# Grouping small tiled matmuls: state reads of two or three batches at once, and W1 pieces as one stream across batches, three at a time in the second group

## The chip, the cores and the metric

The kernel runs on one core of one Trainium2 chip. The metric is device time in microseconds (us) of that core, as a median of several executions. "Span" is the length of the one execution that the profiler recorded; it is a little shorter than the timed runs. In the profiles PE is TensorE, PEld its weight loads, DVE VectorE, ACT ScalarE and POOL GpSimd. A bank is one of the PSUM buffers into which TensorE writes; an eviction is another engine's copy out of it, after which the bank is free again.

## The reference, cut to what matters

```python
# x: (B=8, H=8, S=512, D=64), state: (8, 8, Ns=32, 64), w_in: (512, 2048), w_out: (2048, 512)
a     = softmax(x @ state^T / 8)            # per batch and head, 512 x 32
xread = a @ state                           # 512 x 64
a2    = softmax(state @ x^T / 8)            # 32 x 512
sread = a2 @ x                              # 32 x 64: the "state read"
y     = concat([xread, sread], axis=2)      # (8, 8, 544, 64), heads then joined to 512 columns
h     = y @ w_in                            # 4352 x 2048
out   = (h * sigmoid(h)) @ w_out            # 4352 x 512
```

For the rows of `xread`, the kernel never forms `xread`. It forms `W1 = state @ w_in` for each batch (256 x 2048, once the heads are stacked) and then `h = a @ W1`. Making W1 is one small job per batch, and the state read is another. Both use small pieces of the TensorE array. The state reads are kept until the end, where one last block of 256 rows goes through `w_in` and `w_out`.

## The kernel before

The parts that the change and the argument touch (cuts marked):

```python
    psO = ... tile_pool(name="psO", bufs=1, PSUM)     # o0, o1
    psH = ... tile_pool(name="psH", bufs=2, PSUM)     # h1, twice
    psA = ... tile_pool(name="psA", bufs=1, PSUM)     # a0..a3, given out in turn by bank()

    def sread(bs):                    # state read: 32 matmuls of 65 columns for each batch
        ps = psH.tile([128, 512], FP32, tag="h1", name="ps_sr")
        for i, b in enumerate(bs):
            xm_ps[b] = ps[:, ds(132 * i, 132)]
            for hg in range(2):
                for c in range(4):
                    for s in range(4):
                        # ... cut
                        nc.tensor.matmul(
                            xm_ps[b][ds(32 * s, 32), ds(66 * hg + odd, 65)],
                            exp_nat[b, hg][:, c, s, :],
                            x_rows[b % NX][:, ds(at, 65)],
                            start=(c == 0), stop=(c == 3),
                            tile_position=(0, 32 * s), skip_group_check=True)

    def sread_out(b):                 # its eviction: 4 reciprocals and a product on DVE
        # ... cut

    def w1_mms(b, cols, new=bank):    # one piece is 512 columns of W1: 8 matmuls into 2 banks
        # ... cut
        for f, n in cols:
            for hg in range(2):
                pss[f, hg] = new([128, 512], FP32, "ps_w1")
            for s in range(4):
                for hg in range(2):
                    h = HEAD_OF_SLOT[hg][s]
                    r = 64 * (h % 2)
                    nc.tensor.matmul(
                        pss[f, hg][ds(32 * s, 32), 0:n],
                        stT[ds(r, 64), b, h // 2, s % 2, :],
                        w_in_sb[ds(r, 64), h // 2, ds(f, n)],
                        start=True, stop=True,
                        tile_position=(r, 32 * s), skip_group_check=True)
        return pss

    for b in range(1, B):
        n = b + 1
        m = n + 1
        # ... cut
        for tt in range(4):           # 4 blocks of 128 rows
            for ft in range(NFT):     # 16 steps of G2: o += g @ w_out, a full-size matmul
                at = (tt, ft)
                # ... cut: the h matmuls (G1), loads, casts, transposes
                if n < B and at == (1, 6 if b == 1 else 4):     # the first group
                    if m < B:
                        scores_t(m)
                    pss = w1_mms(n, [(0, 512), (512, 512)])
                    sread((0, 1, 2) if b == 1 else (n,))
                    if m < B:
                        exps_t(m)
                        nc.scalar.activation(warm[:], busy[:, 0:1], func=SILU, bias=0.0)
                    w1_out(n, [(0, 512)], both, pss)
                    for i in (0, 1, 2) if b == 1 else (n,):
                        sread_out(i)
                    w1_out(n, [(512, 512)], both, pss)
                # ... cut
                if n < B:
                    if at == (2, 8):                            # the second group
                        w1_chunks(n, (2, 3), both)
                # ... cut
                G2(b, tt, ft)
```

So each of batches 1 to 6 interrupts the full-size matmuls twice. The first group is eight transposed score matmuls (64 x 32 pieces of the array), two W1 pieces (64 x 32 as well) and a state read (128 x 32 pieces). Batch 1 reads three batches at once, and batch 6 has no scores. The second group is two W1 pieces.

The softmax here doesn't subtract the row's maximum and nothing guards it: scores larger than these inputs give would overflow.

## Time and profile before

| | before |
|---|---|
| time, median of 3 runs | 214.66 us (214.51 to 214.76) |
| span of the profile | 212.8 us |
| PE busy | 97% |
| ACT, DVE busy | 66%, 36% |

From the profile's page of the kernel before, part 1 (busy us, share of the span, instructions) and part 4 (the chain of work that ended last, by engine and then by line):

```profile
PE 206.4 (97%) x1575; PEld 96.6 (45%) x1575; DVE 77.0 (36%) x171; ACT 139.4 (66%) x244; POOL 39.9 (19%) x62
...
PE 90%; DVE 4%; DMA 2%; ACT 2%; issue 0%; SPq 0%
```

The chain is TensorE almost throughout. Whatever shortens the stream of TensorE shortens the kernel, and a lighter DVE or ACT alone does not.

The next lines are from the timeline of PE in the kernel before. The columns are start, length, engine, line, operation, output and inputs, array pieces used, shape, and count of the merged run. The first block holds both groups of batch 2 with the full-size matmuls around them; after it come only the marks at which the groups of the next batches begin.

```profile
70.75 2.32 PE L559 MATMUL o<-w_out_sb,g 128*128 128x512 bf16 x10
73.00 0.41 PE L330 MATMUL ps_scT<-xT,stT 64*32 64x512 bf16 x8
73.23 0.62 PE L464 MATMUL ps_w<-w_in_sb,stT 64*32 64x512 bf16 x16
73.77 0.43 PE L416 MATMUL ps_sr<-x_rows,e 128*32 128x65 bf16 x32
74.14 4.49 PE L559 MATMUL o<-w_out_sb,g 128*128 128x512 bf16 x20
78.56 0.62 PE L464 MATMUL ps_w<-w_in_sb,stT 64*32 64x512 bf16 x16
79.11 2.12 PE L559 MATMUL o<-w_out_sb,g 128*128 128x512 bf16 x9
...
95.62 0.41 PE L330 MATMUL ps_scT<-xT,stT 64*32 64x512 bf16 x8
...
118.24 0.41 PE L330 MATMUL ps_scT<-xT,stT 64*32 64x512 bf16 x8
...
140.86 0.41 PE L330 MATMUL ps_scT<-xT,stT 64*32 64x512 bf16 x8
```

Read starts, not lengths. Matmuls are pipelined, so the length of a run includes the last one's latency and overlaps what follows: a single full-size matmul is recorded with 0.38 us, though the next starts 0.216 us after it. Full-size matmuls start 0.216 us apart. The ten that begin at 70.75 would be followed by another at 70.75 + 10 x 0.216 = 72.91. Instead the scores start at 73.00 and the next full-size matmul at 74.14, so the first group takes 1.23 us out of the stream. The twenty from 74.14 end their turn at 78.46, W1 starts at 78.56 and full-size matmuls are back at 79.11, so the second group takes 0.65 us. Two W1 pieces need only 2 x 0.216 = 0.43 us of array time, as the eight matmuls of a piece run side by side (the eight scores, of the same shape, take 73.00 to 73.23).

A second place matters, batch 1, where three batches are read together and the second group waits. From the timelines of PE and then of DVE in the kernel before:

```profile
46.13 0.59 PE L518 MATMUL h<-aT,W 128*128 128x512 bf16 x2
46.56 0.63 PE L304 MATMUL ps_sc<-stT,xT 128*128 128x64 bf16 x16
47.03 2.32 PE L559 MATMUL o<-w_out_sb,g 128*128 128x512 bf16 x10
...
50.15 0.96 PE L416 MATMUL ps_sr<-x_rows,exp_nat 128*32 128x65 bf16 x96
51.04 4.06 PE L559 MATMUL o<-w_out_sb,g 128*128 128x512 bf16 x18
55.03 0.41 PE L464 MATMUL ps_w<-w_in_sb,stT 64*32 64x512 bf16 x8
56.11 0.41 PE L464 MATMUL ps_w<-w_in_sb,stT 64*32 64x512 bf16 x8 [0.68 <-DVE W L158]
```

```profile
51.97 0.68 DVE L158 CAST W<-ps_w 128x512 bf16<-128x512 f32 x1
52.57 0.69 DVE L432 RECIPROCAL rc<-ps_sr 32x2 f32<-32x2 f32 x4
...
55.17 0.29 DVE L433 TENSOR_TENSOR xm<-ps_sr,rc 128x128 bf16<-128x128 f32 x1
55.38 0.68 DVE L158 CAST W<-ps_w 128x512 bf16<-128x512 f32 x1
```

Three reads together took 50.15 to 51.04 = 0.89 us, a single one 73.77 to 74.14 = 0.37 us. So a batch costs 0.26 us and the read as such 0.11 us. The bracket on the last PE line says that PE sat idle for 0.68 us until a DVE eviction freed a bank. Measured by starts, 55.03 + 0.216 = 55.25 was the due time and 56.11 the real one: 0.86 us lost. Small matmuls that use the *whole* array (scores of batch 2, 128 x 64) start exactly where the next full-size one was due (46.13 + 2 x 0.216 = 46.56). There is no gap ahead of them.

### The profile page before, as it was taken

How to read it: one execution, taken by the hardware profiler on the slowest of the kernel's cores; microseconds unless marked ns; L12 is line 12 of the kernel's file. 1: busy time of each engine (PE TensorE's matmuls, PEld its weight loads, DVE VectorE, ACT ScalarE, POOL GpSimd, SP SyncE). 2: the span in 40 equal slices, each digit the busy share in tenths (PEclk: the TensorE clock that was granted, in tenths of full speed). 3: DMA queues.
4: the chain of work that ended last, by engine and by line, in shares of the span. 5: the costliest groups of instructions: out<-in, count | busy, mean ns of one | idle time of the engine just before them, and what ended most of it. 6: DMA issues, size and time to landing. Idle time of an engine off the chain costs nothing.

```text
span 212.8 us, 3896 instructions
## 1 busy us (share of the span) xinstructions
PE 206.4 (97%) x1575; PEld 96.6 (45%) x1575; DVE 77.0 (36%) x171; ACT 139.4 (66%) x244; POOL 39.9 (19%) x62
## 2 busy tenths in 40 slices
PE   7899999999899999999999999999999999999993
PEld 2443354445344434444444444443444444466653
DVE  3851268738921255115610661045212406100011
ACT  3865677899377876697669955995776366644410
POOL 8682116405120402021200301000200000000000
PEclk9999999999999999999999999999999999999999
DMA  5999999993469358454756573115311111011112
GB/s 189 195 207 204 286 261 350 286 284 108 85 157 270 125 114 163 124 158 108 194 79 219 79 180 99 49 52 105 99 49 46 62 49 54 0 49 49 52 49 99
DMA packets 42930, 28.66 MB, mean 135 GB/s; under 512 B 28064, under 2 KB 37792, under 8 KB 42912
## 3 DMA queue, kind: packets, MB, share of 16 engines
q1 hardware_dynamic: 36720, 20.65, 36.8%
q0 software_dynamic: 5904, 7.64, 17.3%
q8 instruction: 12, 0.20, 0.4%
q10 hardware_dynamic: 288, 0.13, 0.2%
q14 instruction: 6, 0.05, 0.1%
HBM read 17.43 MB, written 8.91 MB: 124 GB/s over the span
## 4 chain that ended last, share of the span: by engine, by line
PE 90%; DVE 4%; DMA 2%; ACT 2%; issue 0%; SPq 0%
PE o L559 48%; PE h L518 26%; PE ps_w L464 4%; PE h L539 3%; PE o_a L559 3%; DMA x_f<-in_x_dram 2%; PE o_part L581 2%; DVE W L158 1%; PE ps_sr L416 1%; DVE rc L432 1%; PE ps_scT L330 1%; PE ps_busy L164 1%; ACT L318 1%; DVE rs L377 1%; ACT exp_nat L318 1%; PE ps_at L396 0%
## 5 line engine op out<-in xcount | busy, mean ns | idle before, releaser
L559 PE MATMUL o<-w_out_sb,g 128*128 128x512 bf16 x496 | 132.2, 379 | 0.0
L550 ACT ACTIVATE g<-h 128x512 bf16<-128x512 f32 (+1 forms) x143 | 81.3, 573 | 35.3 <-PE h L518 21.2
L559 PEld LDWEIGHTS <-g 128*128 128x128 bf16 x528 | 50.0, 98 | 57.9 <-issue 3.2
L518 PE MATMUL h<-aT,W 128*128 128x512 bf16 x254 | 74.7, 379 | 0.1
L158 DVE COPY o_sb<-o 128x512 f32<-128x512 f32 x15 | 10.4, 691 | 89.5 <-PE o L559 80.9
L518 PEld LDWEIGHTS <-W 128*128 128x128 bf16 x254 | 24.5, 98 | 30.6 <-issue 1.2
L158 DVE CAST W<-ps_w 128x512 bf16<-128x512 f32 (+2 forms) x36 | 22.7, 658 | 26.3 <-PE ps_w L464 26.3
L156 ACT ACTIVATE W<-ps_w 128x512 bf16<-128x512 f32 (+1 forms) x32 | 16.6, 561 | 12.6 <-PE ps_w L464 12.6
L158 POOL CAST x_nat<-x_f 128x512 bf16<-128x512 f32 x24 | 14.5, 646 | 33.6 <-issue 21.7
L156 ACT ACTIVATE o_sb<-o 128x512 f32<-128x512 f32 x16 | 9.5, 596 | 13.2 <-PE o L559 10.0
L360 POOL TENSOR_TENSOR an<-e,rcn 128x512 bf16<-128x512 bf16 x5 | 7.6, 1517 | 50.0 <-DVE rcn L358 50.0
L464 PE MATMUL ps_w<-w_in_sb,stT 64*32 64x512 bf16 (+2 forms) x264 | 10.8, 375 | 0.7 <-DVE W L158 0.7
L559 PE MATMUL o_a<-w_out_sb,g 128*128 128x512 bf16 x32 | 10.0, 379 | 0.0
L539 PE MATMUL h<-xmT,w_in_sb 128*128 128x256 bf16 x64 | 9.6, 273 | 0.0
L539 PEld LDWEIGHTS <-w_in_sb 128*128 128x128 bf16 x64 | 6.3, 98 | 3.9
L164 PE MATMUL ps_busy<-busy 128*128 128x512 bf16 x16 | 5.9, 487 | 1.2 <-DVE warm L171 1.2
L344 ACT ACTIVATE eT<-ps_scT 128x512 bf16<-128x512 f32 x10 | 5.4, 594 | 1.6 <-PE ps_scT L330 1.6
L769 ACT ACT_TABLE_LOAD x5 | 6.4, 1283 | 0.1
L464 PEld LDWEIGHTS <-stT 64*32 64x32 bf16 x264 | 3.1, 89 | 7.0 <-issue 5.1
L380 POOL TENSOR_TENSOR an<-exp_nat,rc 128x512 bf16<-128x512 bf16 x3 | 3.1, 1047 | 15.7 <-ACT eT L344 9.9
L357 DVE TENSOR_REDUCE rs<-e 128x32 f32<-128x1024 bf16 x5 | 6.0, 1207 | 0.0
L432 DVE RECIPROCAL rc<-ps_sr 32x2 f32<-32x2 f32 x32 | 5.2, 164 | 0.3
(76 smaller groups left out, 103.7 us busy)
## 6 DMA issues: line engine op xcount, KB each, us to landing
out_dram<-o_sb SPq DMA_DIRECT2D x33, 256.0 KB, 2.5
x_f<-in_x_dram SPq DMA_DIRECT2D x4, 1024.0 KB, 6.0
x_f<-in_x_dram POOLq DMA_DIRECT2D x2, 1024.0 KB, 11.7
w_in_sb<-in_moe_w_in_dram POOLq DMA_DIRECT2D x3, 512.0 KB, 9.9
x_f<-in_x_dram SPq DMA_DIRECT2D x2, 512.0 KB, 4.8
w_out_sb<-in_moe_w_out_dram POOLq DMA_DIRECT2D x4, 256.0 KB, 11.8
w_out_sb<-in_moe_w_out_dram POOLq DMA_DIRECT2D x2, 512.0 KB, 11.9
x_f<-in_x_dram POOLq DMA_DIRECT2D x2, 512.0 KB, 14.6
```

Source lines behind the costliest of these rows:

```text
L156: nc.scalar.activation(dst, src, func=COPY, bias=0.0)
L158: eng.tensor_copy(dst, src)
L164: nc.tensor.matmul(ps[:], busy[:, 0:128], busy[:], start=True, stop=True, skip_group_check=True)
L357: nc.vector.tensor_reduce(rs[:], e2[b][:], axis=AX, op=ADD)
L360: eng.tensor_tensor(a[:, hg], e2[b][:, hg], rc[:, hg].to_broadcast([128, 4, 4, NS]), op=MULT)
L432: nc.vector.reciprocal(rc[q, :], src)
L464: nc.tensor.matmul(pss[f, hg][ds(32 * s, 32), 0:n], stT[ds(r, 64), b, h // 2, s % 2, :], w_in_sb[ds(r, 64), h // 2, ds(f, n)], start=True, ...
L518: nc.tensor.matmul(h_ps[k][:], W1[b][:, hg, ds(128 * ft, 128)], aT[b][:, hg, :, :], start=(hg == 0), stop=(hg == 1), skip_group_check=True,)
L539: nc.tensor.matmul(ps[:, 0:256], w_in_sb[:, kt, ds(128 * ft, 128)], xmT[:, :, kt].rearrange("p t n b -> p t (n b)"), start=(kt == 0), stop ...
L550: nc.scalar.activation(g[:, 0:n], ps[:, 0:n], func=SILU, bias=0.0)
L559: nc.tensor.matmul(outs[tt][:], gt[b * NFT + ft][:, ds(128 * tt, 128)], w_out_sb[:, ft, :], start=(ft == 0), stop=(ft == NFT - 1), skip_gr ...
L769: nc.scalar.activation(warm[:], busy[:, 0:1], func=SILU, bias=0.0)
```

## The change

The intent is to interrupt the full-size stream less often for the same small work. The 24 W1 pieces of batches 2 to 7 are made as one queue, two in every first group and three in a second group, so that only four batches need a second group. The third piece takes the two `h1` banks. The state reads of batches 3 to 7 are done as 3, 4, 5 in batch 4 and 6, 7 in batch 6. One more `e2` buffer keeps the exponentials until then.

```diff
+SREAD_AT = {1: (0, 1, 2), 4: (3, 4, 5), 6: (6, 7)}
 ... cut
-    e2pool = ctx.enter_context(tc.tile_pool(name="e2pool", bufs=3))
+    e2pool = ctx.enter_context(tc.tile_pool(name="e2pool", bufs=4))
 ... cut
+    pieces = [(i, [(512 * c, 512)]) for i in range(2, B) for c in range(4)]
+
+    def w1_next(k, new=bank):
+        done = []
+        for _ in range(k):
+            i, cols = pieces.pop(0)
+            done.append((i, cols, both, w1_mms(i, cols, new)))
+        return done
 ... cut
-                    pss = w1_mms(n, [(0, 512), (512, 512)])
-                    sread((0, 1, 2) if b == 1 else (n,))
+                    pss = w1_next(2)
+                    srs = SREAD_AT.get(b, ())
+                    if srs:
+                        sread(srs)
 ... cut
-                    w1_out(n, [(0, 512)], both, pss)
-                    for i in (0, 1, 2) if b == 1 else (n,):
+                    w1_out(*pss[0])
+                    for i in srs:
                         sread_out(i)
-                    w1_out(n, [(512, 512)], both, pss)
+                    w1_out(*pss[1])
 ... cut
-                    if at == (2, 8):
-                        w1_chunks(n, (2, 3), both)
+                    if at == (2, 8) and b in (1, 2, 4, 5):
+                        pss = w1_next(2) + w1_next(1, new_h)
+                        for i in (2, 0, 1):
+                            w1_out(*pss[i])
```

## The prediction

> **What bounds the kernel.** TensorE. The page gives PE 97% of the 212.8 us span, and the chain that ended last is 90% PE. In the timeline of PE, batches 1 to 6 repeat every 22.6 us (the eight score matmuls start at 73.00, 95.62, 118.24, 140.86). Full-size matmuls start 0.216 us apart, so the 96 of a batch (32 for h, 64 for o) take 20.74 us. The other 1.89 us are two interruptions by tiled matmuls. ACT (66%) and DVE (36%) have slack, and the granted clock is full, so only PE's own stream is worth counting.
>
> **Prices, from the timeline of PE in batch 2.** Group one: the next full matmul was due at 72.91; scores start 73.00, W1 73.23, state read 73.77, full matmuls again at 74.14: 1.23 us. Group two: due 78.46, W1 starts 78.56, full again 79.11: 0.65 us for two W1 pieces. A piece is eight matmuls of 512 columns that run side by side, so 0.216 us. That leaves, as estimates from these numbers, 0.10 us to enter a group and 0.11 us to leave it, about 0.21 us per group. A state read of one batch is 0.37 us; in batch 1 three batches read together take 0.89 us (50.15 to 51.04), so 0.26 us per batch and 0.11 us once per read, for the change of tile shape. The Trainium skill, "TensorEngine Tiling (Array Packing)", section Key Properties, says that changing the tiling mode drains TensorE; these gaps agree with it.
>
> **What the change does.** No matmul is added or removed: still 24 W1 pieces in batches 1 to 6 and eight state reads.
> - Group two goes from six times two pieces to four times three (batches 1, 2, 4, 5). Batches 3 and 6 lose it: -2 x 0.65 = -1.31 us. Four groups gain a piece: +4 x 0.216 = +0.86 us. Net -0.44 us.
> - The reads of batches 2, 3 and 5 go (-3 x 0.37 = -1.11 us); batch 4 reads three and batch 6 two (+3 x 0.26 = +0.78 us). Net -0.33 us.
> - Sum -0.77 us, all on PE and so all on the chain.
>
> **What could collide.** Three read evictions on DVE in batch 4 take about 2.8 us (0.94 each) and hold back the second W1 eviction. Estimated from batch 5's times it ends about 4.8 us after the group begins; group two begins 5.56 us after, so nothing waits. In batch 1 it does wait (W1 at 55.03, second half at 56.11 behind a DVE eviction, about 0.86 us lost); neither the order nor the banks there change, so I expect that loss to stay. The third piece uses the two h banks, evicted first, before h wants them about 2 us later. The fourth e2 buffer lets batch 6's exponentials be written while batches 3 to 5 wait; no new wait.
>
> **Prediction.** 213.9 us, range 213.4 to 214.5 (about -0.36%). Faster by over 2%: 0.5%; within 2%: 99%; slower by over 2%: 0.5%.
>
> **What would show it.** Batch 3's period about 0.37+0.65 = 1.0 us shorter (21.6 us); batch 6 about 0.4 shorter; batches 2 and 5 0.15 shorter; batch 4 longer by 0.52+0.22 = 0.74; batch 1 longer by 0.22. Read of three in batch 4 takes 0.89 us. Third piece 0.216 us. Batch 1's wait for DVE stays near 0.7 to 0.9 us.
>
> **What would make it wrong.** A W1 stall in batch 4 like batch 1's (+0.3 to 0.9 us, the gain gone); the third piece in the h banks waiting for the read's eviction, or h waiting for the piece's; or the batch 1 stall vanishing (0.8 us more gain). If the drain depends on what is in flight, each of five saved switches may be worth 0 to 0.2 us rather than 0.11 to 0.21.

## The result and the profile after

| | before | after |
|---|---|---|
| median | 214.58 us (the 3 runs above and one more) | 213.89 us (4 runs, 213.73 to 214.01) |
| ratio, 95% interval | | 0.9967 (0.9949 to 0.9984) |
| span of the profile | 212.8 us | 212.0 us |

The change is within 2%, but the interval lies wholly below 1.

From the profile's page of the kernel after, parts 1 and 4:

```profile
PE 206.1 (97%) x1575; PEld 96.9 (46%) x1575; DVE 77.3 (36%) x171; ACT 139.2 (66%) x244; POOL 39.5 (19%) x62
...
PE 92%; DVE 4%; ACT 1%; issue 0%
```

PE has 1575 matmuls in both kernels, and its busy share is unchanged, though 0.8 us of span are gone. The saving was made of gaps that the busy figure hardly shows. In the matmul records of the two traces, the array's shape changes 30 times in the six batches before and 23 times after.

From the timeline of PE in the kernel after, batch 2, then the first group of batch 3, then both groups of batch 4:

```profile
70.93 2.32 PE L560 MATMUL o<-w_out_sb,g 128*128 128x512 bf16 x10
73.18 0.41 PE L331 MATMUL ps_scT<-xT,stT 64*32 64x512 bf16 x8
73.41 0.61 PE L465 MATMUL ps_w<-w_in_sb,stT 64*32 64x512 bf16 x16
73.96 4.49 PE L560 MATMUL o<-w_out_sb,g 128*128 128x512 bf16 x20
78.38 0.84 PE L465 MATMUL ps_w<-w_in_sb,stT 64*32 64x512 bf16 x24
79.15 2.12 PE L560 MATMUL o<-w_out_sb,g 128*128 128x512 bf16 x9
...
95.66 0.41 PE L331 MATMUL ps_scT<-xT,stT 64*32 64x512 bf16 x8
95.88 0.61 PE L465 MATMUL ps_w<-w_in_sb,stT 64*32 64x512 bf16 x16
96.43 6.43 PE L560 MATMUL o<-w_out_sb,g 128*128 128x512 bf16 x29
...
117.25 0.41 PE L331 MATMUL ps_scT<-xT,stT 64*32 64x512 bf16 x8
...
118.03 0.96 PE L417 MATMUL ps_sr<-x_rows,e 128*32 128x65 bf16 x96
118.92 4.49 PE L560 MATMUL o<-w_out_sb,g 128*128 128x512 bf16 x20
123.34 0.84 PE L465 MATMUL ps_w<-w_in_sb,stT 64*32 64x512 bf16 x24
124.11 2.12 PE L560 MATMUL o<-w_out_sb,g 128*128 128x512 bf16 x9
...
140.62 0.41 PE L331 MATMUL ps_scT<-xT,stT 64*32 64x512 bf16 x8
```

The second group now lasts 78.38 to 79.15 = 0.77 us with three pieces, against 0.55 us with two: the third costs 0.22 us. In batch 3 the 29 full-size matmuls from 96.43 run through the place where the second group was. The read of three in batch 4 took 118.03 to 118.92 = 0.89 us, and its second group followed without a wait.

The length of each batch, from mark to mark (scores to scores for batches 1 to 4, first W1 to first W1 for batch 5, first W1 of batch 6 to the first h matmul of the last block for batch 6):

| batch | before | after | difference | predicted |
|---|---|---|---|---|
| 1 | 23.70 | 23.93 | +0.23 | +0.22 |
| 2 | 22.62 | 22.48 | -0.14 | -0.15 |
| 3 | 22.62 | 21.59 | -1.03 | -1.0 |
| 4 | 22.62 | 23.37 | +0.75 | +0.74 |
| 5 | 22.39 | 22.25 | -0.14 | -0.15 |
| 6 | 21.92 | 21.52 | -0.40 | -0.4 |

### The profile page after: what moved, and what is told of

It is laid out like the page before. It is cut to its first block, busy times and chain, and to the rows that moved or that the text cites. A ratio compares the mean times of both kernels' runs of the same rounds, so it can differ in the third digit from the quotient of the medians.

```text
span 212.0 us, 3895 instructions
## 1 busy us (share of the span) xinstructions
PE 206.1 (97%) x1575; PEld 96.9 (46%) x1575; DVE 77.3 (36%) x171; ACT 139.2 (66%) x244; POOL 39.5 (19%) x62
## 4 chain that ended last, share of the span: by engine, by line
PE 92%; DVE 4%; ACT 1%; issue 0%
PE o L560 48%; PE h L519 26%; PE ps_w L465 4%; PE h L540 3%; PE o_a L560 3%; PE ps_busy L165 3%; PE o_part L582 2%; DVE W L159 1%; DVE rc L433 1%; PE ps_xt L252 1%; PE ps_sr L417 1%; PE ps_scT L331 1%; PE ps_sc L305 1%; ACT L319 1%; DVE rs L378 1%; PE ps_at L397 0%
## 5 line engine op out<-in xcount | busy, mean ns | idle before, releaser
L165 PE MATMUL ps_busy<-busy 128*128 128x512 bf16 x16 | 6.4, 521 | 1.2 <-DVE warm L172 1.2
```

Source lines behind the costliest of these rows:

```text
L165: nc.tensor.matmul(ps[:], busy[:, 0:128], busy[:], start=True, stop=True, skip_group_check=True)
```

## The experiments

Every kernel below gave a correct result. The timed medians scatter by several tenths of a us, and part of that lies ahead of everything discussed here. In the eleven profiles the first transposed score matmul of batch 1 starts anywhere from 49.20 to 49.92 us. One reason can be seen in the latest of them, from the timeline of PE in the repeat of the changed kernel; the bracket says that PE waited for a load of `w_in`:

```profile
10.04 0.36 PE L465 MATMUL ps_w<-w_in_sb,stT 64*32 64x384 bf16 x8 [0.44 <-DMA w_in_sb<-in_moe_w_in_dram]
```

So the table also gives the *middle stage*: from the first transposed score matmul of batch 1 to the first h matmul of the last block (`h<-xmT`), read from the timeline of PE. All that is edited lies inside it.

| run | first mark, us | last mark, us | middle stage, us | median, us | before, us | ratio (95% interval) |
|---|---|---|---|---|---|---|
| before | 49.30 | 185.40 | 136.10 | | | |
| after | 49.25 | 184.61 | 135.36 | 213.89 | 214.58 | 0.9967 (0.9949 to 0.9984) |
| e1_reads_only | 49.35 | 185.17 | 135.82 | 214.38 | 214.79 | 0.9987 (0.9975 to 1.0) |
| e2_w1_only | 49.20 | 184.86 | 135.66 | 214.09 | 214.79 | 0.9971 (0.9959 to 0.9984) |
| e3_split_groups | 49.31 | 186.06 | 136.75 | 215.23 | 214.79 | 1.0024 (1.0011 to 1.0038) |
| e4_mixed_reads | 49.48 | 185.51 | 136.03 | 214.59 | 214.79 | 0.9995 (0.9983 to 1.0008) |
| e5_again | 49.92 | 185.28 | 135.36 | 214.08 | 214.57 | 0.9976 (0.9964 to 0.9989) |
| e6_evict_w1_first | 49.62 | 184.76 | 135.14 | 213.48 | 214.57 | 0.9949 (0.9936 to 0.9963) |
| e7_two_three_three | 49.61 | 184.29 | 134.68 | 213.31 | 214.57 | 0.9937 (0.9925 to 0.995) |
| e8_both | 49.28 | 183.76 | 134.48 | 213.08 | 214.72 | 0.9926 (0.9912 to 0.994) |
| e9_two_three_three_again | 49.34 | 184.02 | 134.68 | 213.2 | 214.72 | 0.9934 (0.9922 to 0.9946) |

The same kernel run twice gave the same middle stage to the last digit (135.36 twice, 134.68 twice), while its spans differed by 0.6 and 0.2 us. That is why the trace decides here and the medians only confirm. The kernel before has one profile; its batches 2, 3 and 4 agree to the last digit (22.62). The pages of e1 to e4 count 1550 or 1551 matmuls, but 1575 weight loads like all others: records are missing there, not matmuls.

The theory is that every change of the array's shape (full to 64 x 32, 64 x 32 to 128 x 32, and back) costs TensorE a gap of about 0.1 us, and that the change saved such gaps. The rivals are that the gain came from fewer evictions or waits per group, from lighter DVE or DMA work in some batches, or from a fixed cost of the read itself.

### e1_reads_only: the grouping of the reads alone

```diff
 # against before
+SREAD_AT = {1: (0, 1, 2), 4: (3, 4, 5), 6: (6, 7)}
-    e2pool = ... bufs=3
+    e2pool = ... bufs=4
-                    sread((0, 1, 2) if b == 1 else (n,))
+                    srs = SREAD_AT.get(b, ())
+                    if srs:
+                        sread(srs)
-                    for i in (0, 1, 2) if b == 1 else (n,):
+                    for i in srs:
```

> Only the grouping of the state reads; W1 groups as before. Theory (each switch of the array's shape costs TensorE a fixed gap): three reads of one batch fewer, each 0.11 us of fixed cost, so -0.33 us in the trace; batch 4's read 0.89 us, batches 2, 3 and 5 0.37 us shorter, second groups unchanged at 0.65 us. Rival (the gain came from the W1 stream or from lighter DVE and DMA work in some batches): near 0, or more than 0.5 us.

Measured: the middle stage fell by 0.28 us (136.10 to 135.82). Batches 2, 3 and 5 became 0.35 to 0.36 us shorter each and batch 4 0.53 us longer. Timed, the ratio is 0.9987, whose interval just reaches 1. The size agrees with the theory to 0.05 us.

### e2_w1_only: the W1 stream alone

```diff
 # against after
-SREAD_AT = {1: (0, 1, 2), 4: (3, 4, 5), 6: (6, 7)}
+SREAD_AT = {1: (0, 1, 2), 2: (3,), 3: (4,), 4: (5,), 5: (6,), 6: (7,)}
-    e2pool = ... bufs=4
+    e2pool = ... bufs=3
```

> Only the W1 stream; state reads one batch at a time as before. Theory: two second groups fewer, 0.21 us each, so -0.44 us in the trace; the second groups cost 0.87 us in batches 1 (beside its wait), 2, 4, 5 and none in 3 and 6. With the reads-only run it adds up to the whole change, -0.77 us. Rival: the parts do not add up, as one of them hides the other's wait.

Measured: the middle stage fell by 0.44 us (136.10 to 135.66), as expected. With the reads alone that makes 0.28 + 0.44 = 0.72 us, against 0.74 us for the whole change: the parts add up. The timed median was 0.70 us lower, more than the trace gives, and its interval (0.9959 to 0.9984) holds the trace's figure.

### e3_split_groups: the same pieces in six more groups

```diff
 # against after
-                    if at == (2, 8) and b in (1, 2, 4, 5):
-                        pss = w1_next(2) + w1_next(1, new_h)
+                    if b in (2, 4, 5) and at in ((2, 8), (2, 9)):
+                        held = (held if at == (2, 9) else []) + w1_next(1)
+                    if at == (2, 8) and b == 1 or at == (2, 10) and b in (2, 4, 5):
+                        pss = (w1_next(2) if b == 1 else held) + w1_next(1, new_h)
```

> The changed kernel, with the second group of batches 2, 4 and 5 split into three groups of one W1 piece, one full-size matmul between them: the same matmuls, evictions in the same order, six more groups. Theory: six more entries and exits at 0.21 us, +1.27 us over the changed kernel, so about 0.5 us slower than the kernel before. Rival (the gain is fewer evictions or semaphore waits per group, not the switch): under 0.3 us over the changed kernel.

Measured: the middle stage rose by 1.39 us over the changed kernel (135.36 to 136.75), 0.23 us for each of the six added groups, and the kernel became slower than before (1.0024, interval above 1). By the code, the number of matmuls and evictions and the order of the evictions are those of the changed kernel, so the rival of fewer evictions falls. From the timeline of PE in this run, batch 2:

```profile
78.44 0.41 PE L465 MATMUL ps_w<-w_in_sb,stT 64*32 64x512 bf16 x8
78.78 0.39 PE L560 MATMUL o<-w_out_sb,g 128*128 128x512 bf16 x1
79.10 0.41 PE L465 MATMUL ps_w<-w_in_sb,stT 64*32 64x512 bf16 x8
79.44 0.39 PE L560 MATMUL o<-w_out_sb,g 128*128 128x512 bf16 x1
```

One full-size matmul between two pieces takes 0.32 us from 78.78 to 79.10 instead of 0.216, and one piece 0.34 us from 79.10 to 79.44 instead of 0.216. There is 0.10 us on the way in and 0.12 us on the way out at these crossings, and no wait for another engine is marked.

### e4_mixed_reads: more changes of shape inside the same groups

```diff
 # against after (sread gains an argument that picks one batch of a common bank)
-                    pss = w1_next(2)
                     srs = SREAD_AT.get(b, ())
-                    if srs:
-                        sread(srs)
+                    if b in (4, 6):
+                        sread(srs, 0)
+                        pss = w1_next(1)
+                        sread(srs, 1)
+                        pss = pss + w1_next(1)
+                        if len(srs) == 3:
+                            sread(srs, 2)
+                    else:
+                        pss = w1_next(2)
+                        if srs:
+                            sread(srs)
```

> The changed kernel, with batch 4's group ordered read, W1, read, W1, read and batch 6's read, W1, read, W1: no more groups, six more changes between the W1 shape and the read shape inside them. Theory: each change of shape costs 0.11 us, +0.66 us over the changed kernel, so about 0.1 us faster than before. Rival (only going to and from the full array costs, or a read costs a fixed 0.11 us for another reason, such as its first weight load): 0 to +0.2 us over the changed kernel, or up to +0.33.

Measured: the middle stage rose by 0.67 us over the changed kernel (135.36 to 136.03), 0.11 us for each of the six added changes of shape. From the timeline of PE in this run, the first group of batch 4:

```profile
117.49 0.41 PE L331 MATMUL ps_scT<-xT,stT 64*32 64x512 bf16 x8
117.83 0.43 PE L423 MATMUL ps_sr<-x_rows,e 128*32 128x65 bf16 x32
118.19 0.41 PE L471 MATMUL ps_w<-w_in_sb,stT 64*32 64x512 bf16 x8
118.53 0.43 PE L423 MATMUL ps_sr<-x_rows,e 128*32 128x65 bf16 x32
118.89 0.41 PE L471 MATMUL ps_w<-w_in_sb,stT 64*32 64x512 bf16 x8
```

Eight tiled matmuls followed by another shape take 0.34 us (118.19 to 118.53). Followed by their own shape they take 0.22 to 0.23 us (73.18 to 73.41 after). A read followed by W1 takes 0.36 us (117.83 to 118.19), nearly as much as one followed by the full array (0.37 us). So it is not the full array that costs, nor the read as such, but the change of shape. The gap at each change is shown; what inside the array makes it, no run tells.

The weight loads narrow it. From the timeline of all engines in the kernel before, first group of batch 3, its weight loads (PEld) and W1's matmuls:

```profile
95.62 0.11 PEld L330 LDWEIGHTS <-stT 64*32 64x32 bf16 x8 [0.42 <-issue]
95.65 0.32 PEld L464 LDWEIGHTS <-stT 64*32 64x32 bf16 x16
95.85 0.61 PE L464 MATMUL ps_w<-w_in_sb,stT 64*32 64x512 bf16 x16
...
96.39 0.31 PEld L416 LDWEIGHTS <-e 128*32 128x32 bf16 x32 [0.42 <-issue]
```

W1 follows matmuls of its own shape, and its loads begin 0.20 us ahead of its first matmul. The scores and the read come with a change of shape, and their loads begin only with their first matmuls (95.62 and 96.39), after 0.42 us without a load. At each of the 30 changes of shape of that trace the first load is at most 0.02 us ahead; in the full-size stream it is 0.21 us ahead in the median. So loading ahead stops at a change of shape. Whether the late load makes the gap (one is recorded with about 0.10 us) or both wait for the same thing was not tested.

### e5_again: the changed kernel as a base on another chip job

```diff
 # the changed kernel, no edit
```

> The changed kernel again, on the chip of the two runs beside it, as their base. Theory: 0.77 us faster than before by the trace's sums, ratio near 0.9964.

Measured: ratio 0.9976 (0.9964 to 0.9989), middle stage 135.36 us as in the first profile. The expected ratio of 0.9964 is the edge of the interval. The wait for `w_in` shown above fell into this run's start-up.

### e6_evict_w1_first: the wait in batch 1, tried from the order of DVE

```diff
 # against after
                     w1_out(*pss[0])
+                    if b == 1:
+                        w1_out(*pss[1])
                     for i in srs:
                         sread_out(i)
-                    w1_out(*pss[1])
+                    if b != 1:
+                        w1_out(*pss[1])
```

> The changed kernel, with batch 1's second W1 eviction ahead of the three read evictions on DVE. Theory (batch 1's second group waits because the eviction that frees its second pair of banks stands behind 2.8 us of read evictions): the second piece starts at about 55.2 instead of 56.07, but the third piece needs the h bank that the reads hold until about 56.0, so it now waits, and only 0.1 to 0.2 us is gained. Rival (the wait has another cause, such as the transposes or ACT): no change, 56.07 stays.

Measured: the middle stage fell by 0.22 us (135.36 to 135.14). From the timeline of PE in this run, batch 1's second group:

```profile
55.35 0.82 PE L465 MATMUL ps_w<-w_in_sb,stT 64*32 64x512 bf16 x17
56.45 0.41 PE L465 MATMUL ps_w<-w_in_sb,stT 64*32 64x512 bf16 x7 [0.28 <-DVE xm L434]
```

Two pieces and the first matmul of the third now run without a stop, and the wait has moved to the third piece's second bank, which the reads' own eviction (`xm`) held. The wait is thus DVE's queue of read evictions, whichever bank stands behind it. The timed gain over the repeat of the changed kernel is larger (213.48 against 214.08). In the two profiled executions, 0.30 us of the 0.5 us between the spans lie ahead of the middle stage (first marks 49.62 and 49.92).

### e7_two_three_three: fewer read evictions ahead of that group

```diff
 # against after
-SREAD_AT = {1: (0, 1, 2), 4: (3, 4, 5), 6: (6, 7)}
+SREAD_AT = {1: (0, 1), 3: (2, 3, 4), 6: (5, 6, 7)}
```

> The changed kernel, with the state reads as batches 0 and 1 in batch 1, 2 to 4 in batch 3, 5 to 7 in batch 6: as many reads, but one read eviction (0.94 us of DVE) fewer before batch 1's second group, and the reads of three where no second group follows. Theory: the eviction that frees the banks ends near 55.0, before the second piece wants them at 55.2, so the whole 0.86 us wait goes: 0.8 to 0.9 us faster than the changed kernel, about 1.6 us faster than before (ratio near 0.992). Rival: the wait stays or another takes its place, under 0.3 us.

Measured: the middle stage fell by 0.68 us (135.36 to 134.68), less than the 0.8 to 0.9 expected; ratio to before 0.9937, where about 0.992 was expected. From the timeline of PE in this run:

```profile
55.06 1.05 PE L465 MATMUL ps_w<-w_in_sb,stT 64*32 64x512 bf16 x24
56.05 1.25 PE L560 MATMUL o<-w_out_sb,g 128*128 128x512 bf16 x5
```

The group lasts 0.99 us, and three pieces without a wait take 0.77. So 0.22 us of the wait were left. The expectation had moved DVE's eviction forward by one read eviction (0.94 us) but not the group that waits for it: with two batches instead of three the read itself is 0.26 us shorter on TensorE, and the second group comes that much sooner. The eviction that frees its banks ends at 55.35 (54.75 plus 0.60 on DVE) and the second piece is due at 55.06 + 0.216 = 55.28. That is 0.07 us too late. The rest is about what PE needed after such an eviction in the kernel before, where it ended at 55.98 by the same reckoning and the piece started at 56.11, 0.13 us later.

### e8_both and e9_two_three_three_again

```diff
 # e8 against after: the edits of e6 and e7 together; e9 is e7 again
```

> The two previous edits together: reads in twos and threes (two, three, three) and batch 1's second W1 eviction ahead of its read evictions. In the two-three-three run the second group of batch 1 still lasted 0.99 us (55.06 to 56.05) against 0.77 us for three undisturbed pieces, as the eviction that frees its banks ended at 55.35, after the second piece wanted them (55.28). Theory: with W1 first, the banks are free near 53.5 and the h bank near 55.35, before the third piece wants it at 55.49, so the group lasts 0.77 us: 0.22 us less from the first scores to the end than in the two-three-three run. Rival: some other wait in that group remains, no change.

> The two-three-three kernel again, on the chip of the run beside it: group of 0.99 us in batch 1, about 162.0 us from the first scores to the end, 0.7 us less than the changed kernel.

Measured: e9 repeated e7's middle stage of 134.68 us; its group in batch 1 took 0.97 us (54.80 to 55.77). e8 has 134.48 us, 0.20 less, and its group takes 0.78 us:

```profile
54.74 0.84 PE L465 MATMUL ps_w<-w_in_sb,stT 64*32 64x512 bf16 x24
55.52 1.69 PE L560 MATMUL o<-w_out_sb,g 128*128 128x512 bf16 x7
```

(timeline of PE in e8). The wait in batch 1 is gone. e8 is the fastest kernel: 213.08 us, ratio to before 0.9926 (0.9912 to 0.994), and its middle stage is 0.88 us shorter than the changed kernel's. The timed difference between e8 and e9 themselves (0.12 us) is within their scatter; that step is shown by the trace.

## Why the prediction was right

- **What bounds the kernel.** It named TensorE's stream. Every tenth saved or added inside the six batches came out at the end: the middle stage fell by 0.74 us, the span by 0.8 and the median by 0.69.
- **The price of a group.** 0.21 us was worked out from two gaps of one batch. Six added groups in e3 cost 0.23 us each. The exit is 0.12 us and not 0.11, and the term was 10% small.
- **The price of a read.** 0.11 us per read fixed and 0.26 us per batch were taken from the difference of two reads. In the changed kernel the read of three took 0.89 us, as predicted, and six added shape changes in e4 cost 0.11 us each. The Trainium skill, "TensorEngine Tiling (Array Packing)", section Key Properties, says that changing the tiling mode drains TensorE. Both experiments agree with it, though none shows the drain itself: the price follows the changes of shape, not the number of matmuls, evictions or groups. The control in batch 1, with small matmuls on the full array and no gap, agrees too.
- **The sum.** -0.44 us for W1 measured -0.44 (e2); -0.33 us for the reads measured -0.28 (e1); -0.77 us in all measured -0.74. Seven changes of shape fewer (30 to 23) make that 0.11 us each, as in e3 (1.39 us for twelve more) and e4 (0.67 us for six more). That the median came to 213.89 where 213.9 was predicted is partly luck: the interval of the timed ratio is about 0.4 us wide on either side.
- **What could collide.** Nothing new did. The wait of batch 1 stayed (0.68 us of idle PE in both profiles). In batch 4 the margin was predicted from an eviction that ends 4.8 us after the group begins and a second group 5.56 us after it. Both came later: the eviction ended 5.26 us after (on the timeline of DVE it started at 121.91 and took about 0.6), since DVE first waited 0.39 us for the longer read, and the second group came 6.09 us after, as the read of three is 0.52 us longer. The margin, 0.83 us, was much as predicted (0.76), because both ends had moved. The prediction had missed both moves, so that the margin held was luck; the same oversight did show in the expectation for e7.
- **What it left on the table.** The prediction saw 0.86 us lost in batch 1 and rightly said that the change would not touch it. That wait was worth more than the change itself, and two small edits (e8) took it away.

## What to carry to other kernels

Where TensorE is the bound and small tiled matmuls interrupt its full-size stream, count changes of array shape, not matmuls: order the work so that equal shapes stand together and save it up until a bank is full, then price each change by the gap between due and real starts in the timeline. Gathering such work also gathers its evictions on another engine, so look at what stands behind them in that engine's queue before the next group needs a bank. When one end of such a race is moved, check whether the other end moves as well.

## What the Trainium skill lacked or had wrong

- "TensorEngine Tiling (Array Packing)", Key Properties, says that a change of tiling mode drains TensorE and gives no price. Here it was 0.09 to 0.10 us into a tiled shape and 0.11 to 0.12 us out of one, and 0.11 us on average between two tiled shapes or back (e3: 0.23 us for a pair; e4: 0.67 us for six). It does not say either whether weights are still loaded ahead over such a change; here the first load was at most 0.02 us ahead at all 30 changes, against 0.21 us in the full-size stream.
- "TensorE: Matmul & The Clock Gate", section Back-to-back issue gap, gives about 131 ns for each matmul of 512 columns in a sustained stream of weight loads and matmuls, and says that 216 ns over-counts it. Here, with a weight load for every matmul at the full clock, starts were 0.216 us apart throughout (two h matmuls and what follows: 46.13 to 46.56). So the 216 ns, which the section gives for an isolated matmul, held in a stream too, and the 131 ns did not.
- "Perfetto Trace Analysis" warns of the busy share of matmuls and sends the reader to the gaps between slices (its word for recorded instructions), but lacks that a short gap leaves none: matmuls recorded with 0.38 us start 0.216 us apart, so a gap of 0.10 us lies hidden under the record before it. PE's busy share was 97% before and after while 0.8 us of span went; these gaps have to be read from starts.
